# One query head group's transpose and the number of exp tiles in flight: a two-layer spectral and attention kernel

## The chip, the core and the metric

The kernel runs on one core of a Trainium2 chip. The metric is the device time of one execution in microseconds (us); the kernel before has a median of 1332.8 us over three runs (1332.57 to 1332.93). Engines are named as the profile names them: PE is TensorE (matmul), PEld its weight load, DVE is VectorE, ACT is ScalarE, POOL is GpSimd, SP is SyncE, which here only issues DMAs.

## What is computed

A residual stream of 2048 rows by 512 columns goes through two pairs of layers. A spectral layer normalises the rows, takes a 2-D real Fourier transform, multiplies by a complex filter and transforms back. An attention layer has 32 query heads of 16 columns each, and one key and one value head that all of them share.

```python
def _B_ref(x, wq, wk, wv, wo):
    H = 32; Dh = D // H
    q = (x @ wq).reshape(B, S, H, Dh).transpose(0, 2, 1, 3)
    k = x @ wk
    v = x @ wv
    scores = einsum("bhqd,bkd->bhqk", q, k) * (Dh ** -0.5)
    p = softmax(scores, axis=-1)
    o = einsum("bhqk,bkd->bhqd", p, v)
    return o.transpose(0, 2, 1, 3).reshape(B, S, H * Dh) @ wo

x = x + _A_ref(_layernorm(x), A_w_r, A_w_i)   # spectral
x = x + _B_ref(_layernorm(x), B_wq, B_wk, B_wv, B_wo)
x = x + _A_ref(_layernorm(x), A_w_r, A_w_i)
x = x + _B_ref(_layernorm(x), B_wq, B_wk, B_wv, B_wo)
```

## The kernel before

**Units of attention.** The 2048 queries are cut into four query blocks `qb` of 512. In each, the 32 heads are cut into four groups `g` of eight, and each group into two halves `par` of four heads: 4 x 4 x 2 = 32 *blocks* per layer. A block has 16 key chunks `kc` of 128 keys times 4 heads `h`, so 64 *units*. A unit is one score matmul (`scores`, L1341: 32 rows of the array, one 32-row strip per head, 128 keys by 512 queries), an exp of the 128x512 scores, and a product with the values (`pv`, L1363: 128 keys by 32 columns, one 32-column strip per head). Scores of heads in different strips run side by side, as do four products. Of the 32 columns of a value operand 16 are the values and 16 are constant, so that the product also gives the softmax's denominator.

**Who does the exp.** Two units at a time (a *pair*) go to ACT, which writes a 128x1024 tile `e` (`exp`, L1346). Single units go to DVE: `p1` (L1353) turns the score into the bits of a bf16 number by one multiply and add, an approximation of the exponential; four such units fill a tile, and two *phases* (`phase`, L1357 on POOL, L1359 on DVE) make shifted copies of it, so that such a unit has three products with weighted values instead of one.

**End of a block.** When all products of a block are in, DVE evacuates the accumulator with a transpose of its 32x32 squares (`evac`, L1370). After the second half of a group, DVE takes the reciprocals of the denominators (`recip`, L1375) and multiplies (`mul`, L1381), which leaves `on`, 128 queries' lanes by 512, in bf16. `on` has to be transposed back, in 32x32 squares, into `OT`, the operand of the output projection (`proj`, L1406). For all groups but the last of a layer this is `norm_dma` (L1392): four copies into a DRAM tile `onw` (L1401) and a DMA transpose out of it (L1402), all on SP's queue. For the last group it is `norm` (L1390), a transpose on DVE.

**Who decides the order.** All instructions are emitted by a planner (`Plan`), which keeps a clock for PE, ACT, DVE and POOL, with costs written in the code (`ACT_EXP = 908.0`, `DVE_P1 = 600.0`, and so on), and at each step emits the work that can start soonest. The order is therefore fixed when the program is built, per engine; on the chip each engine takes its own list in order and waits by semaphores. Which units go to ACT and which to DVE is decided there too, by whichever engine the plan sees going idle first (`deadline`, `do_scores`). A pair goes to ACT only if fewer than `self.bufs["ACT"]` exp tiles are live, that is, written or about to be, with products still to come:

```python
if kind == "ACT":
    if self.live["ACT"] >= self.bufs["ACT"] or self.slot_free("sa") is None:
        return False
```

`bufs["ACT"]` is `E_BUFS = 8` while a layer begins, and `E_LATE = 12` as soon as all values of the layer are there (L882). Up to `T_BUFS = 4` of DVE's tiles may be live. Within that, `peek` (L621) chooses heads for ACT's pair and DVE's unit so that they lie in different strips.

**Memory.** Exp tiles come from a ring of 21 fixed SBUF tiles `e2` (L975), which the spectral layer also uses: for its transposed input (`xt`, by DMA in the second pair, L1085), for the inverse transform's intermediate `V`, and for `Dz`, the sums and differences that `radix_d` (L1199) makes and the inverse transform's matmuls (`inv`, L1210) read.

Of the kernel before, what the change touches and what calls it, by code (L numbers as in the profile page):

```python
# [8 lines left out]
ACT = mybir.ActivationFunctionType  # L9
ALU = mybir.AluOpType  # L10
P = 128
BF = mybir.dt.bfloat16
# [40 lines left out]
    return tabs  # L53


def radix2(nc, o, x, piece):

    nc.vector.tensor_tensor(out=o, in0=x[:, 0:2, :], in1=x[:, 2:4, :], op=ALU.subtract if piece else ALU.add)


def radix4(nc, sd, x, half, o, piece):
# [53 lines left out]
class Plan:  # L115
# [12 lines left out]
    PORT = True  # L128
    POOL_LAG = 2600.0
    E_BUFS = 8  # L130
    E_LATE = 12
    T_BUFS = 4
    WIN = 3413.0
    WARM = 3500.0
# [11 lines left out]
    PATIENT = 1000.0  # L146
    URGE = 150.0
    TURN = 7000.0
    OUT_TURN = 25000.0
    EARLY_SD = 0  # L150
    STARVED = 12000.0

# [442 lines left out]
class Attn:  # L595
# [74 lines left out]
    def done(self, b, slot, end):  # L670
        p, em = self.plan, self.em
        qb, g, par = self.blocks[b]
        self.left.discard(b)
        m = Mark("PE", end, slot)
        ev = p.add("DVE", 630.0, [m], lambda k: em.evac(self, b, slot), give=(m,), prio=-3)
        self.evac[b] = self.evac_last = ev
        if par == 0:
            return
        tail = 0.0 if b >= len(self.blocks) - 2 else 5000.0
        rc = p.add("DVE", 260.0, [ev, self.evac[b - 1]], lambda k: em.recip(self, b), lazy=tail)  # L680
        mu = p.add("DVE", 600.0, [rc], lambda k: em.mul(self, b), lazy=tail, port=True)
        if b < len(self.blocks) - 2:
            no = Mark("DMA", None)

            def turned(k):
                em.norm_dma(self, b)
                no.end = k.end + p.OUT_TURN

            mu.then = turned
        else:  # L690
            no = p.add("DVE", 626.0, [mu], lambda k: em.norm(self, b), lazy=tail)
        self.evac[b] = no
        if g == 3:
            self.layer.close_rows(qb, [self.evac[8 * qb + 2 * i + 1] for i in range(4)])


class Layer:
# [83 lines left out]

    def add_middle(self):
        p, em = self.plan, self.em
        p.bufs["ACT"] = p.E_BUFS
        self.mid, self.fil = [], []
        for u in range(4):
            evs, two = [], u in self.two

            if two:
                outs = [((0, 2), (0, 1), 0), ((1, 3), (0, 1), 2)]  # L790
            else:
                outs = [((0, 1, 2, 3), (0, 1), 0), ((0, 1, 2, 3), (2, 3), 2)]
            if u % 2:
                outs = [(ts, (k,), o + i) for ts, ks, o in outs for i, k in enumerate(ks)]
            for ts, ks, o in outs:
                base, prev = None, []
                for t in ts:
                    deps, take = [self.g_done[t]] + prev, None
                    if not prev:
                        deps = deps + (self.gate if len(ks) == 2 else self.mm1_done[T - 1])  # L800
                        take = "sa" if len(ks) == 2 else "b"
                    k = p.add("PE", 434.0 * len(ks), deps, lambda k, u=u, ks=ks, t=t, ts=ts, base=base:
                              em.mid(self, u, ks, t, ts, (base or k).slot), take=take, order=10 + u)
                    base, prev = base or k, [k]
                evs.append(p.add("ACT", 909.0 if len(ks) == 2 else 482.0, prev, lambda k, u=u, o=o, n=len(ks), base=base:
                                 em.mid_evac(self, u, o, n, base.slot), give=(base,), order=10 + u))
            if two:
                evs = [self.pieces((600.0, 600.0), evs, lambda i, u=u: em.turn(self, u, i), 10 + u)]
            if u == 3 and not two:
                a = p.add("DVE", 1733.0, evs[:2], lambda k, u=u: em.filt(self, u, 0, 2), order=10 + u, port=True)  # L810
                mu = p.add("DVE", 1733.0, evs[2:] + [a], lambda k, u=u: em.filt(self, u, 2, 4), order=10 + u, port=True)
            else:
                mu = p.add("DVE", 3466.0, evs, lambda k, u=u: em.filt(self, u, 0, 4), order=10 + u, port=True)
            self.fil.append(mu)
            self.mid.append(self.pieces((600.0, 600.0), [mu], lambda i, u=u: em.radix_d(self, u, i), 26 if self.direct else 10 + u))
# [5 lines left out]
    def add_back(self):  # L821
        p, em, at = self.plan, self.em, self.at
        left = [T]
        for t in range(T):
            o = 20 + 10 * t
            cs = []
            for b in range(2):
                es = []
                for j in range(2):
                    if t == 0 and not self.direct:  # L830
# [3 lines left out]
                                  lambda k, t=t, b=b, j=j, m=m: em.inv(self, t, b, j, m.slot, (1,)), order=o)  # L834
                    elif t == 0:
# [3 lines left out]
                                  lambda k, b=b, j=j, m=m: em.inv0(self, b, j, m.slot, 1), order=o)  # L839
# [8 lines left out]
            for j in range(0, R, w):  # L848
                key, ks = ("b", t, j), []
                for i, r in enumerate(range(j, j + w)):  # L850
# [4 lines left out]
                    if put:  # L855
                        c = p.add("ACT", 482.0, [y], lambda k, t=t, r=r, y=y: em.put_x(t, r, y.slot), order=o + 1)
                        b = p.add("DVE", 795.0, [y], lambda k, key=key, i=i, t=t, r=r, w=w, y=y:
                                  em.bn(self, key, i, (t, r), w, y.slot), order=o + 2)
# [3 lines left out]
                    z = p.add("DVE", 597.0, [y], lambda k, t=t, r=r, y=y: em.add_x(t, r, y.slot), give=(y,), order=o + 1)  # L862
# [6 lines left out]
                for a in range(j, j + w, 2):  # L869
                    ap = [p.add("DVE", 323.0, [nb], lambda k, t=t, r=r: em.apply(self, t, r), order=o + 3) for r in (a, a + 1)]  # L870
                    x = p.add("PE", 560.0, ap, lambda k, s, t=t, a=a: em.tr_n(self, t, a, k.slot, s), parts=2, cols=1024.0, take="b", order=o + 4)
                    te.append(p.add(*self.flex(t, 893.0, 602.0), [x],
                                    lambda k, t=t, a=a, x=x: em.trn_evac(self, t, a, x.slot, k.eng), give=(x,), order=o + 4))
# [4 lines left out]
            def v_got(k, t=t):  # L878
                at.v_ready[t] = k.end + p.LAT[k.eng]
                left[0] -= 1  # L880
                if left[0] == 0:
                    p.bufs["ACT"] = p.E_LATE  # L882
                if left[0] == self.EARLY:
                    at.dve_on = True
                    at.dve_from = k.end - 2000.0
# [61 lines left out]
class Emit:  # L947


    def __init__(self, ctx, tc, ins, out):  # L950
        nc = self.nc = tc.nc
        A_x, self.w_r, self.w_i, B_wq, B_wk, B_wv, B_wo = ins
        mk = lambda nm, b=1, **kw: ctx.enter_context(tc.tile_pool(name=nm, bufs=b, **kw))
        const = mk("const")
# [17 lines left out]
        self.part = const.tile([P, 2], F32, name="part")  # L972
        self.wv = const.tile([P, NC, DH], BF, name="wv")
        self.tc = tc
        self.e2 = [const.tile([P, 1024], BF, name=f"e2_{i}") for i in range(21)]  # L975
        self.idle, self.home, self.writer = list(range(21)), {}, {}
        self.WO = const.tile([P, 4, D], BF, name="WO")
        self.junk = const.tile([P, 512], BF, name="junk")
        self.eps = const.tile([P, 1], F32, name="eps")
# [197 lines left out]
    def turn(self, L, u, piece):  # L1177
        if piece == 0:
            L.sd_of[("x", u)] = self.t4([4, 512])
        radix2(self.nc, L.sd_of[("x", u)][:, 2 * piece:2 * piece + 2, :], L.X[u], piece)  # L1180
        if piece:
            L.X[u] = L.sd_of.pop(("x", u))

# [14 lines left out]

    def radix_d(self, L, u, piece):  # L1199
        if piece == 0:  # L1200
            L.Dz[u] = [[self.t2([2, 512]), 4] for _ in range(2)]
            for z, _ in L.Dz[u]:
                self.writer.pop(self.home[id(z)][0], None)
        radix2(self.nc, L.Dz[u][piece][0], L.X[u], piece)

    def load_it(self, L, t):
        L.IT[t] = self.t4([4, 640], tag="it", bufs=2)
# [2 lines left out]
    def inv(self, L, t, b, j, slot, ks):  # L1210
        for v in range(T):
            if v <= t + 1 and v not in L.IT:
                self.load_it(L, v)
        ps = self.ps(slot).rearrange("p (u x) -> p u x", u=2)
        for k in ks:
            u = 2 * j + k
            for a in range(2):
                for i in range(2):
                    w = 128 * (3 - (t * a + i) % 4)
                    z = L.Dz[u][t % 2][0][:, a, 256 * i + 128 * b:256 * i + 128 * b + 128]  # L1220
                    self.nc.tensor.matmul(ps[:, k, :], lhsT=z, rhs=L.IT[t][:, u, w:w + 256], start=(a == 0 and i == 0),
                                          stop=(a == 1 and i == 1), skip_group_check=True)
            d = L.Dz[u][t % 2]
            d[1] -= 1
            if d[1] == 0:
                self.free2(d[0])

    def inv0(self, L, b, j, slot, k):

# [159 lines left out]
            at.OT[qb] = self.t4([4, 512])  # L1389
        self.nc.vector.transpose(out=at.OT[qb][:, g, :], in_=on.rearrange("p a h d -> p (a h d)"))  # L1390

    def norm_dma(self, at, b):  # L1392

        qb, g, par = at.blocks[b]
        on = at.raw.pop((qb, g))
        if g == 0:
            at.OT[qb] = self.t4([4, 512])
        way = self.way.tile([512, P], BF, name="onw", tag="onw")
        rows = way.rearrange("(a q) (h c) -> h q a c", q=32, c=32)
        for h in range(4):  # L1400
            self.nc.sync.dma_start(out=rows[h], in_=on[32 * h:32 * h + 32].rearrange("p a h d -> p a (h d)"))  # L1401
        self.nc.sync.dma_start_transpose(out=at.OT[qb][:, g:g + 1, :], in_=way)  # L1402

    def proj(self, at, t, r, slot, g0, g1):
        for g in range(g0, min(g1, 4)):
            self.nc.tensor.matmul(self.ps(slot), lhsT=at.OT[t][:, g, r * P:(r + 1) * P], rhs=self.WO[:, g, :],  # L1406
# [90 lines left out]
```

## Time and profile before

| | |
|---|---|
| median of three runs | 1332.8 us |
| profiled execution | 1332.57 us |
| its span, first to last instruction | 1330.8 us |
| POOL busy | 842.0 us (63%) |
| granted TensorE clock | 1.00 throughout |
| DMA | 33.05 MB; 6 to 9% of the 16 engines in most of the attention |
| first attention layer | from about 100 us to 675 us |
| second attention layer | from about 765 us to 1322 us |

The profile is of one execution. The busy time of an engine counts an instruction from its start to its end; consecutive instructions of DVE and ACT overlap by some tenths of a microsecond, so the time that an instruction takes away from its engine is the step from its start to the start of the next. In the rows of the tile view, the numbers behind the count are the shortest, median and longest duration in ns, then first and last start in us. The waits list who waited, at which line, for whom. The spectral layer at the start and between the attention layers leaves all engines partly idle; at 133 to 660 us and 800 to 1300 us PE, DVE and ACT are all near full.

### The profile page before, as it was taken

How to read it: one execution, taken by the hardware profiler on the slowest of the kernel's cores; microseconds unless marked ns; L12 is line 12 of the kernel's file. 1: busy time of each engine (PE TensorE's matmuls, PEld its weight loads, DVE VectorE, ACT ScalarE, POOL GpSimd, SP SyncE). 2: the span in 40 equal slices, each digit the busy share in tenths (PEclk: the TensorE clock that was granted, in tenths of full speed). 3: DMA queues.
4: the chain of work that ended last, by engine and by line, in shares of the span. 5: the costliest groups of instructions: out<-in, count | busy, mean ns of one | idle time of the engine just before them, and what ended most of it. 6: DMA issues, size and time to landing. Idle time of an engine off the chain costs nothing. (4 is left out here: it accounts for less than half of the span.)

```text
span 1330.8 us, 31765 instructions
## 1 busy us (share of the span) xinstructions
PE 1291.0 (97%) x12968; PEld 438.2 (33%) x13032; DVE 1273.3 (96%) x2280; ACT 1226.4 (92%) x1396; POOL 842.0 (63%) x826
## 2 busy tenths in 40 slices
PE   9999999999999999999999999999999999999998
PEld 4643222222222223332256422223222322322232
DVE  6998999999999999999979999999999999999998
ACT  6478999999999999999954899999999999999996
POOL 0004787857777667766720067887677867786785
PEclk9999999999999999999999999999999999999999
DMA  9100000010000100010051000000100010000001
GB/s 294 41 1 1 10 9 10 10 41 10 5 7 12 39 9 10 9 41 10 9 166 41 1 1 9 10 10 9 25 10 10 10 25 6 9 14 22 5 9 25
DMA packets 108722, 33.05 MB, mean 25 GB/s; under 512 B 88352, under 2 KB 107296, under 8 KB 108576
## 3 DMA queue, kind: packets, MB, share of 16 engines
q1 hardware_dynamic: 108288, 30.46, 10.0%
q8 instruction: 102, 1.67, 0.5%
q10 hardware_dynamic: 288, 0.56, 0.1%
q14 instruction: 44, 0.36, 0.1%
HBM read 17.89 MB, written 7.60 MB: 19 GB/s over the span
## 5 line engine op out<-in xcount | busy, mean ns | idle before, releaser
L1341 PEld LDWEIGHTS <-KA 32*128 32x128 bf16 x2048 | 87.6, 91 | 234.1 <-issue 222.9
L1341 PEld LDWEIGHTS <-KB 32*128 32x128 bf16 x2048 | 85.2, 91 | 229.7 <-issue 224.1
L1363 PEld LDWEIGHTS <-vs_116 128*32 128x32 bf16 x2474 | 98.3, 94 | 97.2 <-issue 90.8
L1363 PEld LDWEIGHTS <-vs_117 128*32 128x32 bf16 x1622 | 97.7, 94 | 62.8 <-issue 60.6
L1363 PEld LDWEIGHTS <-vs_118 128*32 128x32 bf16 x1622 | 71.0, 93 | 75.6 <-issue 72.8
L1363 PEld LDWEIGHTS <-vs_119 128*32 128x32 bf16 x1622 | 72.0, 94 | 65.5 <-issue 57.5
L1357 POOL INT64_ADD w_1388<-w_1387 x1 | 1.0, 1039 | 110.5 <-DVE w_1387 L1353 110.5
L1357 POOL INT64_ADD w_11001<-w_11000 x1 | 1.0, 1037 | 98.3 <-PE b_69 L1341 98.3
L1050 DVE BATCH_NORM_STATS2 st<-x_sb 128x6 f32<-128x512 bf16 x52 | 35.4, 681 | 4.1 <-DMA x_sb<-in_A_x_dram 3.6
L1346 ACT ACTIVATE e_8_92<-sa_65 128x1024 bf16<-128x1024 f32 x32 | 35.5, 1110 | 2.4 <-PE sa_64 L1341 1.6
L1346 ACT ACTIVATE e_6_90<-sa_64 128x1024 bf16<-128x1024 f32 x33 | 36.5, 1106 | 0.0
L1346 ACT ACTIVATE e_13_97<-sa_65 128x1024 bf16<-128x1024 f32 x31 | 34.7, 1118 | 1.6 <-PE sa_64 L1341 1.6
L1346 ACT ACTIVATE e_1_85<-sa_64 128x1024 bf16<-128x1024 f32 x32 | 35.4, 1107 | 0.0
L1346 ACT ACTIVATE e_5_89<-sa_65 128x1024 bf16<-128x1024 f32 x30 | 33.5, 1118 | 1.6 <-PE sa_64 L1341 1.6
L1346 ACT ACTIVATE e_12_96<-sa_65 128x1024 bf16<-128x1024 f32 x31 | 34.1, 1100 | 0.9 <-PE b_69 L1341 0.8
L1346 ACT ACTIVATE e_19_103<-sa_65 128x1024 bf16<-128x1024 f32 x31 | 34.7, 1121 | 0.1
L1346 ACT ACTIVATE e_10_94<-sa_65 128x1024 bf16<-128x1024 f32 x30 | 33.2, 1106 | 1.7 <-PE sa_64 L1341 1.6
L1346 ACT ACTIVATE e_18_102<-sa_64 128x1024 bf16<-128x1024 f32 x31 | 34.6, 1115 | 0.1
L1346 ACT ACTIVATE e_2_86<-sa_65 128x1024 bf16<-128x1024 f32 x30 | 33.5, 1116 | 1.3 <-PE sa_64 L1341 1.0
L1346 ACT ACTIVATE e_9_93<-sa_64 128x1024 bf16<-128x1024 f32 x31 | 34.6, 1115 | 0.1
L1346 ACT ACTIVATE e_7_91<-sa_65 128x1024 bf16<-128x1024 f32 x31 | 34.4, 1110 | 0.1
L1346 ACT ACTIVATE e_15_99<-sa_64 128x1024 bf16<-128x1024 f32 x31 | 34.3, 1107 | 0.1
(4100 smaller groups left out, 6438.4 us busy)
## 6 DMA issues: line engine op xcount, KB each, us to landing
it<-const_IT SPq DMA_DIRECT2D x8, 640.0 KB, 6.1
onw<-on SPq DMA_DIRECT2D x120, 32.0 KB, 1.9
x_sb<-in_A_x_dram SPq DMA_DIRECT2D x4, 512.0 KB, 6.8
out_dram<-x_sb SPq DMA_DIRECT2D x16, 128.0 KB, 1.9
way<-x_sb SPq DMA_DIRECT2D x6, 256.0 KB, 2.4
tab_PH<-const_PH ACTq DMA_DIRECT2D x1, 512.0 KB, 4.9
w_131<-const_FT SPq DMA_DIRECT2D x1, 512.0 KB, 8.8
w_136<-const_FT SPq DMA_DIRECT2D x1, 512.0 KB, 8.4
```

The costliest lines, as they stand in the source:

```text
L1050: self.nc.vector.bn_stats(st, self.ps(slot) if slot else self.x[:, x[1], x[0], :])
L1341: self.nc.tensor.matmul(o, lhsT=KX[rs, kc * P:(kc + 1) * P], rhs=at.QT[qb][rs, g, :], start=True, stop=True, skip_group_check=True)
L1346: self.wrote("ACT", e, self.nc.scalar.activation(out=e, in_=self.ps(slot), func=ACT.Exp, scale=SCALE))
L1357: self.nc.gpsimd.int64_add(t[p][:, 0:n].bitcast(U64), t[0][:, 0:n].bitcast(U64), DELTA[p] * FOUR)
L1363: self.nc.tensor.matmul(self.ps(slot)[32 * h:32 * h + 32, :], lhsT=V[:, kc, :], rhs=rhs, start=first, stop=last, skip_group_check=True)
```

## The change

The description of the change says that the score heads of ACT's pairs and DVE's tiles are chosen so that they lie in different strips. `peek`, which does so, is the same in both kernels. What differs is this. `norm_dma` is gone, and all groups are transposed by `norm` on DVE. `E_LATE` is gone, so that at most 8 exp tiles are live throughout. `Dz` has four tiles of its own (tag `xd`), and the shared ring has 13 tiles. `radix2` takes the whole tile and does the slicing itself.

```diff
-    E_LATE = 12
...
-    OUT_TURN = 25000.0
...
         mu = p.add("DVE", 600.0, [rc], lambda k: em.mul(self, b), lazy=tail, port=True)
-        if b < len(self.blocks) - 2:
-            no = Mark("DMA", None)
-
-            def turned(k):
-                em.norm_dma(self, b)
-                no.end = k.end + p.OUT_TURN
-
-            mu.then = turned
-        else:
-            no = p.add("DVE", 626.0, [mu], lambda k: em.norm(self, b), lazy=tail)
+        no = p.add("DVE", 626.0, [mu], lambda k: em.norm(self, b), lazy=tail)
         self.evac[b] = no
...
-        p.bufs["ACT"] = p.E_BUFS
...
-                if left[0] == 0:
-                    p.bufs["ACT"] = p.E_LATE
...
-        self.e2 = [const.tile([P, 1024], BF, name=f"e2_{i}") for i in range(21)]
-        self.idle, self.home, self.writer = list(range(21)), {}, {}
+        self.e2 = [const.tile([P, 1024], BF, name=f"e2_{i}") for i in range(13)]
+        self.idle, self.home, self.writer = list(range(13)), {}, {}
...
         if piece == 0:
-            L.Dz[u] = [[self.t2([2, 512]), 4] for _ in range(2)]
-            for z, _ in L.Dz[u]:
-                self.writer.pop(self.home[id(z)][0], None)
-        radix2(self.nc, L.Dz[u][piece][0], L.X[u], piece)
+            L.Dz[u] = self.t4([4, 512], tag="xd", bufs=4)
+        radix2(self.nc, L.Dz[u], L.X[u], piece)
...
-    def norm_dma(self, at, b):
-
-        qb, g, par = at.blocks[b]
-        on = at.raw.pop((qb, g))
-        if g == 0:
-            at.OT[qb] = self.t4([4, 512])
-        way = self.way.tile([512, P], BF, name="onw", tag="onw")
-        rows = way.rearrange("(a q) (h c) -> h q a c", q=32, c=32)
-        for h in range(4):
-            self.nc.sync.dma_start(out=rows[h], in_=on[32 * h:32 * h + 32].rearrange("p a h d -> p a (h d)"))
-        self.nc.sync.dma_start_transpose(out=at.OT[qb][:, g:g + 1, :], in_=way)
```

Because the planner's clocks change with the tasks, the whole order of scores, products and exps behind the first change is laid anew in the built program, on every engine.

More of the change, by code (lines that the diff above doesn't have):

```diff
@@ L53, in host_tables, with radix2 @@
     return tabs
-def radix2(nc, o, x, piece):
-    nc.vector.tensor_tensor(out=o, in0=x[:, 0:2, :], in1=x[:, 2:4, :], op=ALU.subtract if piece else ALU.add)
+def radix2(nc, sd, x, piece):
+    nc.vector.tensor_tensor(out=sd[:, 2 * piece:2 * piece + 2, :], in0=x[:, 0:2, :], in1=x[:, 2:4, :],
+                            op=ALU.subtract if piece else ALU.add)
 def radix4(nc, sd, x, half, o, piece):
@@ L1179, in turn @@
             L.sd_of[("x", u)] = self.t4([4, 512])
-        radix2(self.nc, L.sd_of[("x", u)][:, 2 * piece:2 * piece + 2, :], L.X[u], piece)
+        radix2(self.nc, L.sd_of[("x", u)], L.X[u], piece)
         if piece:
@@ L1219, in inv @@
                     w = 128 * (3 - (t * a + i) % 4)
-                    z = L.Dz[u][t % 2][0][:, a, 256 * i + 128 * b:256 * i + 128 * b + 128]
+                    z = L.Dz[u][:, 2 * (t % 2) + a, 256 * i + 128 * b:256 * i + 128 * b + 128]
                     self.nc.tensor.matmul(ps[:, k, :], lhsT=z, rhs=L.IT[t][:, u, w:w + 256], start=(a == 0 and i == 0),
                                           stop=(a == 1 and i == 1), skip_group_check=True)
[L1223 to L1226, printed above, removed]
     def inv0(self, L, b, j, slot, k):
```

## Prediction

> **What bounds the kernel now.** I read the page's busy line first, then the engines' busy times by stage, then the waits of the engine that the change loads.
>
> ```profile
> span 1330.8 us, 31765 instructions
> PE 1291.0 (97%) x12968; PEld 438.2 (33%) x13032; DVE 1273.3 (96%) x2280; ACT 1226.4 (92%) x1396; POOL 842.0 (63%) x826
> ```
>
> Three engines are nearly full, and an average cannot say which is nearest to its limit. So I take the two attention stretches alone (columns: stretch, length, then busy time of PE, PEld, DVE, ACT, POOL, the clock, the DMA share, GB/s):
>
> ```profile
> 140.00:660.00 520.00, 509.12 (x5307) 150.96 (x5329) 511.11 (x873) 517.07 (x572) 385.87 (x378) 1.00 0.09 15
> 800.00:1300.00 500.00, 489.83 (x5201) 147.28 (x5210) 491.03 (x822) 494.75 (x539) 383.02 (x370) 1.00 0.07 12
> ```
>
> VectorE has 520.00 - 511.11 = 8.9 us free in the first and 500.00 - 491.03 = 9.0 us in the second, 17.9 us together. ScalarE is as full (2.9 and 5.3 us free). Here whatever is added to either engine lengthens the stretch, unless it fits into these few microseconds or into work taken from the same engine. Where VectorE's free time goes, its waits say (each row: who, waited for whom, us in total, times, longest):
>
> ```profile
> DVE w_2777 L1285 <- PE b_69 L1325: 1.9, 1, 1.9
> DVE w_8863 L1353 <- PE sa_64 L1341: 1.6, 1, 1.6
> DVE w_14548 L1285 <- PE b_68 L1325: 1.9, 1, 1.9
> ```
>
> The long ones are single stalls in which TensorE makes query tiles (L1325) just ahead of the scores that need them. All VectorE waits in the two stretches add up to 7.1 and 7.8 us.
>
> **The DMA way of the head transpose.** The tile view of `on`, the normalised head group that is to be transposed:
>
> ```profile
> L1401 SPq DMA_DIRECT2D onw<-on x120: 315/489/1557, 145.2 to 1300.7; - x120
> L1381 DVE TENSOR_TENSOR on<-raw,rc x32: 676/682/694, 144.5 to 1322.7; 128x512 bf16<-128x512 f32 x32
> L1390 DVE STREAM_TRANSPOSE w_8479<-on x1: 711/711/711, 676.3 to 676.3; 128x512 bf16<-128x512 bf16 x1
> L1390 DVE STREAM_TRANSPOSE w_17903<-on x1: 712/712/712, 1323.5 to 1323.5; 128x512 bf16<-128x512 bf16 x1
> ```
>
> Of the 32 head groups (16 in each layer), 30 leave by DMA (120 copies, 30 DMA transposes on SP's queue) and 2, the last of each layer, are transposed on VectorE. The copies land in a median 1.9 us, the DMA transposes in 2.4 to 2.8 us, and the waits of TensorE, VectorE and ScalarE name no DMA inside the attention stretches: this path costs the bounding engines nothing today.
>
> **Part 1: 30 transposes return to VectorE.** The price is the step to the next start, not the duration, because VectorE overlaps the end of one instruction with the next. The timeline gives it:
>
> ```profile
> 142.72 0.68 DVE L1353 TENSOR_SCALAR w_1846<-b_68 128x512 uint16<-128x512 f32 x1
> 143.32 0.68 DVE L1353 TENSOR_SCALAR w_1846<-b_66 128x512 uint16<-128x512 f32 x1
> ...
> 660.16 0.71 DVE L1370 STREAM_TRANSPOSE raw<-b_68 128x512 f32<-128x512 f32 x1
> 660.79 0.65 DVE L1353 TENSOR_SCALAR w_9685<-b_69 128x512 uint16<-128x512 f32 x1
> ```
>
> An exp tile on VectorE (L1353) occupies 0.60 us, the evacuating transpose of equal width and duration (L1370) 0.63 us. The L1390 rows themselves are followed by waits, so their own step is not to be had; with 711 ns against 706 I give them 0.63. **30 x 0.63 = 18.9 us**, all in the full stretches. In exchange SP loses 150 DMAs. What stands behind them in its queue (the x blocks' way out and back, the stores) can only be issued sooner; no compute engine waits for those now, so the gain is 0. What this lets through next is nothing: VectorE stays the limit.
>
> One thing is not shown: an SBUF-to-SBUF transpose beside a running GpSimd add. Both L1390 rows ran with GpSimd idle. The rows beside it:
>
> ```profile
> 672.31 1.07 POOL L1357 INT64_ADD w_9851<-w_9849  x1
> 671.90 0.58 DVE L1359 TENSOR_SCALAR w_9889<-w_9888 128x512 uint16<-128x512 uint16 x1
> 672.40 1.12 DVE L1359 TENSOR_SCALAR w_9890<-w_9888 128x512 uint16<-128x512 uint16 x1
> ```
>
> The same 16-bit SBUF operation took 0.58 us once and 1.12 us while a GpSimd add ran to its end. At worst each transpose pays this 0.54 us: 30 x 0.54 = 16.2 us more. At best it pays nothing, as L1370 does (706 ns, step 0.63, in the 51 cases beside an add as in the 7 without), and that value I take, since L1390's 711 ns equals it. It can't be a gain, as the instructions do not exist today. The Trainium skill (VectorE: DVE Perf Modes, section "Two Vector instructions with no wait between them") has a one-input operation read through the interface shared with GpSimd only in a two-port mode; no row here shows which mode L1390 is in.
>
> The rule that speaks against all this is in the same page, sections "The three transpose paths" and "Rules for kernel authors": a 128x128 bf16 transpose takes 311 ns on VectorE and 1309 ns by DMA, and VectorE is called fastest for 32x32 blocks. By it, as an estimate, 30 x 4 x 1.0 = 120 us would be saved. The trace has 0.71 us for four times that width on VectorE and 2.4 us for a DMA landing, so the order of the two is the same, but no engine waits for the DMA and VectorE is full.
>
> **Part 2: 12 exp tiles in flight become 8.** This changes what the planner deals to whom, which the built order tells. Exp pairs on ScalarE (L1346): 1238 before, 1235 after. Exp tiles on VectorE (L1353): 1622 before, 1626 after. VectorE therefore gets 4 x 0.60 = **2.4 us** on top, while ScalarE loses 3 x 0.90 = 2.7 us (0.90 is the usual step between exps), which is off the path once VectorE is longer. This is the surprise of the built order. If the 18.9 us were shared, ScalarE would have to take some 10 pairs more, and each engine would end about 9 us later, at 1342. The planner does the reverse: with at most 8 live exp tiles ScalarE is not fed during the bursts in which VectorE finishes a group. Before, 36 exps had their first use 8 or more pairs later on TensorE; after, none has.
>
> TensorE: 7348 instead of 7340 head products (2 rounds, 0.4 us) and 59 more turns between scores, head products and full-width work. A round steps by 0.215 us, across a turn by 0.31, so 59 x 0.10 = 5.9 us. Warm-up products on zeros fall from 112 to 89, at most 1.7 us back. Net about +5 us, covered by the 21 us that the stretches grow; without that cover it would cost those 5 us.
>
> The last phase adds: VectorE makes 4 of one tile each before, and after one of four and two of two tiles. The two pairs took from 671.90 to 673.52 and the same at 1319, 3.2 us; eight tile widths at 0.50 (the first row's step) are 4.0, so **+0.8**, with -1 and +6 as ends (the whole width at the smallest step seen for the narrow form, or 1.12 us for each).
>
> **Part 3: four private tiles for the inverse transform's input; 13 shared tiles instead of 21.** The built order has the same 20 additions of the same shape. A shared tile comes round after 13 exps and is held for at most 8, so a writer finds it free (if it did not, it would wait one exp step, 0.90 us, each time): 0. The choice of strips by heads that the description names is not touched by the diff, so it brings no time.
>
> **VectorE's stalls.** They move with the plan. Counting TensorE work between VectorE's score tiles, by the steps above, the old order has eight places of 2.0 to 5.9 us, and the trace shows six stalls of 1.2 to 1.9 us; the new order has nine of 2.1 to 4.3 us. I keep 0, with -9 and +9 as ends (half of today's 17.9 us gone, or half as much again).
>
> **Sum.** 18.9 + 2.4 + 0.8 = 22.1 us. The profiled execution took 1332.57 us (span 1330.8 and 1.8 around it), 0.2 below the median of 1332.8. 1332.6 + 22.1 = 1354.7, and beside the median **1355**.
>
> **Rivals.**
> - *VectorE's free time takes it up (the other side).* The place is the 17.9 us in the two stretches, above all the query-tile stalls. For no change, 22.1 - 2.7 = 19.4 us would have to vanish, more than there is. If all of it went, 1336.8; if half, 1346. For: three engines plan anew, and the stalls are the planner's doing. Against: the new order has as many such places. Chance 0.10, of which 0.03 that the price of a transpose is also so much smaller that the time is within 0.2% of before or below.
> - *GpSimd disturbs the transposes.* 1355 + 16 = 1371. For: the 1.12 us row. Against: 711 ns looks like the undisturbed form. Chance 0.08.
> - *Eight in flight starve the rest.* The 36 late uses, held back one exp step each, are 36 x 0.90 = 32 us on ScalarE, which has 22.1 + 2.7 + 8.2 = 33 us free after the change. Should they fall where VectorE waits too, up to a third, some 10 us, is added: 1365. Chance 0.12.
> - *The change does nothing*: excluded by the built order.
>
> **How the numbers follow.** Forecast 0.70: 1348 to 1362. The rivals add 1337 to 1348 below, and 1362 to 1371 above. Leaving out the outer parts of both gives **1343 to 1368**. About 0.2% (2.7 us) is what can be told from no change here: slower 0.97, same 0.02, faster 0.01.
>
> **What would show it.** Right: VectorE 32 transposes at 0.71 us, its busy time near 1295 us and still about 98% of the attention stretches; ScalarE's free time there up by some 20 us; SP's queue nearly empty; each query-block period (141.7 us in layer two) longer by 2.5 to 3 us. Wrong: L1390's successors at 1.2 us, or VectorE with over 30 us free while ScalarE waits for TensorE, or ScalarE still full.

## The result, and the profile after

The changed kernel takes 1346.6 us (median of 4 runs, 1346.21 to 1348.28) against 1332.7 beside it: a ratio of 1.0107 (95% interval 1.0089 to 1.0124), 13.9 us slower. The time lies in the range that was given, on the side that was forecast; the likeliest case, 1355, was 8.4 us too high, and 1346.6 lies below the stretch of 1348 to 1362 that was given 0.70. It is where the rival "VectorE's free time takes it up" stood (1346, "if half"), with a chance of 0.10. The page's span and busy line of the changed kernel:

```profile
span 1344.3 us, 31506 instructions
PE 1303.0 (97%) x12950; PEld 442.1 (33%) x13017; DVE 1291.4 (96%) x2313; ACT 1224.3 (91%) x1393; POOL 843.7 (63%) x827
```

VectorE has 18.1 us more to do than before, ScalarE 2.1 us less. In the two attention stretches (columns as before: stretch, length, busy PE, PEld, DVE, ACT, POOL, clock, DMA share, GB/s):

```profile
140.00:667.00 527.00, 515.19 (x5305) 151.85 (x5324) 517.95 (x887) 515.34 (x570) 385.12 (x378) 1.00 0.03 8
807.00:1313.00 506.00, 495.74 (x5200) 149.61 (x5216) 500.47 (x838) 494.25 (x538) 385.04 (x372) 1.00 0.02 5
```

VectorE is free for 9.05 + 5.53 = 14.6 us (17.9 before), ScalarE for 11.66 + 11.75 = 23.4 us (8.2 before). VectorE has become the fuller of the two, and the room opened on ScalarE. The DMA share is down from 9 and 7% to 3 and 2%: the head groups' way through DRAM is gone.

The tile view of `on` (count, then shortest, median and longest ns) shows the transposes that came in:

```profile
L1362 DVE TENSOR_TENSOR on<-raw,rc x32: 675/682/694, 144.1 to 1337.2; 128x512 bf16<-128x512 f32 x32
L1371 DVE STREAM_TRANSPOSE w_1970<-on x4: 701/702/703, 149.7 to 257.3; 128x512 bf16<-128x512 bf16 x4
...
L1371 DVE STREAM_TRANSPOSE w_11507<-on x4: 701/702/704, 816.3 to 923.9; 128x512 bf16<-128x512 bf16 x4
```

**Where the 13.9 us lie.** To separate work from waiting I give each kind of VectorE instruction its usual step in an unbroken row (exp tile 0.598 for a duration of 0.681, evacuation 0.630, `mul` 0.599, `norm` 0.625, and so on), multiply by the counts, and call the sum VectorE's *list*. What the stretch takes beyond it is the *time above the list*: waits, and steps longer than usual. The stretch is from a layer's first exp tile on VectorE to its last evacuation, both layers together, in the profiled executions (1332.57 and 1346.21 us). All in us:

| | before | after | difference | forecast |
|---|---|---|---|---|
| VectorE's list in the attention | 1084.3 | 1104.9 | +20.6 | +22.1 |
| time above the list | 32.0 | 26.3 | -5.7 | 0 (ends -9 and +9) |
| ahead of the two attention stretches | 205.3 | 204.8 | -0.5 | 0 |
| after the last evacuation | 9.2 | 8.2 | -1.0 | 0 |

(The rounded rows sum to 13.4, against 13.6 of the two profiled executions.) The last row is the output projection's: the last group's transpose is followed by 13 projection matmuls in the trace before and by 7 in the one after, since the new plan does more of them ahead.

So two questions are open: is the list the thing that sets the time, and is the 5.7 us a share that any added work gets back, or chance of the new plan?

### The profile page after: what moved, and what is told of

Its sections match the earlier page's. It is cut to its first block, busy times and chain, and to the rows that moved or that the text cites. A ratio compares the mean times of both kernels' runs of the same rounds, so it can differ in the third digit from the quotient of the medians.

```text
span 1344.3 us, 31506 instructions
## 1 busy us (share of the span) xinstructions
PE 1303.0 (97%) x12950; PEld 442.1 (33%) x13017; DVE 1291.4 (96%) x2313; ACT 1224.3 (91%) x1393; POOL 843.7 (63%) x827
## 4 chain that ended last, share of the span: by engine, by line
ACT 60%; PE 22%; DVE 16%; issue 2%; DVEq 0%; ACTq 0%
ACT e_11_95 L1327 5%; ACT e_0_84 L1327 5%; ACT e_1_85 L1327 5%; ACT e_8_92 L1327 5%; ACT e_6_90 L1327 5%; ACT e_2_86 L1327 5%; ACT e_4_88 L1327 4%; ACT e_10_94 L1327 4%; ACT e_7_91 L1327 4%; ACT e_3_87 L1327 4%; ACT e_12_96 L1327 4%; ACT e_9_93 L1327 4%; ACT e_5_89 L1327 4%; PE b_67 L1344 2%; PE sa_65 L1322 2%
## 5 line engine op out<-in xcount | busy, mean ns | idle before, releaser
L1322 PEld LDWEIGHTS <-KB 32*128 32x128 bf16 x2048 | 88.5, 91 | 228.5 <-issue 221.8
L1344 PEld LDWEIGHTS <-vs_108 128*32 128x32 bf16 x2470 | 102.4, 93 | 97.7 <-issue 90.3
L1344 PEld LDWEIGHTS <-vs_109 128*32 128x32 bf16 x1626 | 97.1, 94 | 70.5 <-issue 69.0
L1344 PEld LDWEIGHTS <-vs_111 128*32 128x32 bf16 x1626 | 74.0, 94 | 79.0 <-issue 74.7
L1344 PEld LDWEIGHTS <-vs_110 128*32 128x32 bf16 x1626 | 71.6, 94 | 75.0 <-issue 70.6
L1327 ACT ACTIVATE e_8_92<-sa_65 128x1024 bf16<-128x1024 f32 x49 | 55.0, 1122 | 4.1 <-PE sa_64 L1322 4.1
L1327 ACT ACTIVATE e_6_90<-sa_65 128x1024 bf16<-128x1024 f32 x50 | 55.7, 1115 | 2.7 <-PE sa_64 L1322 2.5
L1327 ACT ACTIVATE e_7_91<-sa_65 128x1024 bf16<-128x1024 f32 x49 | 55.0, 1121 | 1.2 <-PE sa_64 L1322 1.0
L1327 ACT ACTIVATE e_12_96<-sa_65 128x1024 bf16<-128x1024 f32 x49 | 54.8, 1119 | 1.3 <-PE sa_64 L1322 0.9
L1327 ACT ACTIVATE e_11_95<-sa_64 128x1024 bf16<-128x1024 f32 x50 | 55.9, 1118 | 0.1
L1327 ACT ACTIVATE e_2_86<-sa_65 128x1024 bf16<-128x1024 f32 x46 | 51.8, 1127 | 4.4 <-PE sa_65 L1322 4.4
L1327 ACT ACTIVATE e_9_93<-sa_64 128x1024 bf16<-128x1024 f32 x49 | 54.8, 1118 | 0.8 <-PE b_69 L1322 0.8
L1327 ACT ACTIVATE e_4_88<-sa_65 128x1024 bf16<-128x1024 f32 x46 | 51.5, 1120 | 4.4 <-PE sa_64 L1322 3.5
L1327 ACT ACTIVATE e_3_87<-sa_65 128x1024 bf16<-128x1024 f32 x48 | 53.9, 1124 | 1.5 <-PE b_68 L1322 0.7
L1327 ACT ACTIVATE e_5_89<-sa_64 128x1024 bf16<-128x1024 f32 x49 | 55.0, 1121 | 0.1
L1327 ACT ACTIVATE e_5_89<-sa_65 128x1024 bf16<-128x1024 f32 x47 | 53.2, 1132 | 1.7 <-PE sa_64 L1322 1.4
L1327 ACT ACTIVATE e_2_86<-sa_64 128x1024 bf16<-128x1024 f32 x48 | 54.3, 1131 | 0.1
L1327 ACT ACTIVATE e_10_94<-sa_65 128x1024 bf16<-128x1024 f32 x48 | 54.1, 1128 | 0.0
L1327 ACT ACTIVATE e_0_84<-sa_65 128x1024 bf16<-128x1024 f32 x48 | 53.9, 1123 | 0.1
```

The lines of the kernel that those rows point to most:

```text
L1322: self.nc.tensor.matmul(o, lhsT=KX[rs, kc * P:(kc + 1) * P], rhs=at.QT[qb][rs, g, :], start=True, stop=True, skip_group_check=True)
L1327: self.wrote("ACT", e, self.nc.scalar.activation(out=e, in_=self.ps(slot), func=ACT.Exp, scale=SCALE))
L1344: self.nc.tensor.matmul(self.ps(slot)[32 * h:32 * h + 32, :], lhsT=V[:, kc, :], rhs=rhs, start=first, stop=last, skip_group_check=True)
```

## The experiments

Four theories. **A**: VectorE's list sets the time, and the time above it belongs to each plan. **B**: part of any added work, about a third, vanishes into VectorE's waits. **C**: the transposes carry all of the loss and eight in flight none. **D**: the long query-tile stalls cost nothing, because another wait is right behind them. In the table, units are exp tiles on VectorE and pairs those on ScalarE; the last two columns are measured as above.

| kernel | us | units / pairs | VectorE's list | above it |
|---|---|---|---|---|
| before | 1332.8 | 1622 / 1238 | 1084.3 | 32.0 |
| after | 1346.6 | 1626 / 1235 | 1104.9 | 26.3 |
| 1 transposes alone | 1340.8 | 1610 / 1243 | 1095.4 | 30.0 |
| 2 eight in flight alone | 1340.05 | 1636 / 1230 | 1092.7 | 29.8 |
| 3 extra transposes, old order | 1349.0 | 1622 / 1238 | 1106.1 | 27.5 |
| 4 transposes doubled, new order | 1365.6 | 1626 / 1235 | 1122.7 | 28.3 |
| 5 without the ring change | 1346.6 | 1626 / 1235 | 1104.9 | 26.3 |
| 6 before, query tiles earlier | 1329.5 | 1622 / 1237 | 1081.4 | 28.2 |
| 7 the same, with precedence | 1331.5 | 1612 / 1242 | 1074.9 | 35.8 |
| 8 after, query tiles earlier | 1335.7 | 1624 / 1236 | 1100.8 | 18.8 |
| 9 as 1, query tiles earlier | 1335.2 | 1600 / 1248 | 1086.5 | 34.2 |
| 10 as 2, query tiles earlier | 1334.1 | 1643 / 1227 | 1094.4 | 23.2 |
| 11 nine in flight, query tiles earlier | 1328.0 | 1630 / 1233 | 1086.2 | 23.6 |

The times are medians, the last two columns are of one execution each. Those of 3 and 4 took 1350.6 and 1366.6 us; in them TensorE's granted clock was 0.50 for 3.4 and 13.7 us, which adds some 1.6 and 5.5 us to the last column.

### 1. The transposes alone

The kernel before, with every group transposed on VectorE; 12 stay in flight.

```diff
-        if b < len(self.blocks) - 2:
+        if False:
```

> The kernel before, with every group's transpose on VectorE; 12 exp tiles in flight, 21 ring tiles and the DMA-free rest as before. The built order deals 1610 units to VectorE (1622 before) and 1243 pairs to ScalarE (1238), so VectorE's list grows by 30 x 0.625 - 12 x 0.598 = 11.6 us. Theory A (VectorE's list sets the time, and its stalls are a matter of each plan, zero on average): 1332.7 + 11.6 = 1344, give or take 5 for the stalls. Theory B (a third of whatever is added to VectorE disappears into its stalls, as 22 added gave 14): 1332.7 + 0.64 x 11.6 = 1340. Theory C (the transposes are what costs, and the 12 or 8 in flight do not matter): 1346.6, as the changed kernel.

1340.8 us, ratio 1.0059 (1.0044 to 1.0074): 8.0 us for 30 transposes whose steps sum to 18.75. The planner moved 12 units (7.2 us) off VectorE, so its list grew by only 11.1. This is the sharing that the prediction had worked out as "each engine would end about 9 us later, at 1342" and set aside, because the built order of the whole change doesn't show it. With 12 in flight it happens. A said 1344, give or take 5, and B 1340.

### 2. Eight in flight alone

```diff
-    E_LATE = 12
+    E_LATE = 8
```

> The kernel before with at most 8 exp tiles in flight throughout; transposes by DMA as before. The built order deals 1636 units to VectorE (1622 before) and 1230 pairs to ScalarE (1238): VectorE's list grows by 14 x 0.598 = 8.4 us. Theory A: 1332.7 + 8.4 = 1341, give or take 5. Theory B: 1332.7 + 0.64 x 8.4 = 1338. Theory C: 1333, no change.

1340.05 us, ratio 1.0065 (1.004 to 1.009): 7.2 us. Three executions took 1339.5 to 1340.6 us, the fourth 1347.0 at a mean granted clock of 0.992. C falls; A said 1341 and B 1338. The planner turned 8 pairs into 14 units (8.4 us) for VectorE; its list grew by 8.4. Parts 1 and 2 alone add up to 15.2 us, the whole measured 13.9.

### 3. Extra transposes in the old order

Each of the 30 groups that leave by DMA is also transposed on VectorE into a tile that nobody reads. It is emitted behind `mul`, out of the planner's sight, so the rest of the order stays as it was.

```diff
+        self.spare = const.tile([P, 512], BF, name="spare")
...
+        self.nc.vector.transpose(out=self.spare, in_=on.rearrange("p a h d -> p (a h d)"))
         way = self.way.tile([512, P], BF, name="onw", tag="onw")
```

> The kernel before in its own order, unit for unit, with 30 transposes of the same operand into a tile that nobody reads added to VectorE's list where the DMA way starts; the plan does not know of them. VectorE's list grows by 30 x 0.625 = 18.8 us and nothing else moves. Theory A: 1332.7 + 18.8 = 1351.5 within 2 us. Theory B: 1332.7 + 0.64 x 18.8 = 1345.

1349.0 us, ratio 1.012 (1.0103 to 1.0137), 16.1 us more. The tile view of `on` in this kernel:

```profile
L1399 DVE STREAM_TRANSPOSE spare<-on x30: 711/711/712, 145.7 to 1315.6; 128x512 bf16<-128x512 bf16 x30
L1391 DVE STREAM_TRANSPOSE w<-on x2: 711/711/711, 685.1 to 1341.2; 128x512 bf16<-128x512 bf16 x2
```

The added instructions have the duration of the two that were there before, but they cost more than the 0.625 that was expected for them. Each stands right behind the `mul` whose result it reads. VectorE's timeline at the first of them, before and in this kernel:

```profile
144.51 0.68 DVE L1381 TENSOR_TENSOR on<-raw,rc 128x512 bf16<-128x512 f32 x1
145.11 0.68 DVE L1353 TENSOR_SCALAR w_1906<-b_68 128x512 uint16<-128x512 f32 x1
```

```profile
144.98 0.68 DVE L1382 TENSOR_TENSOR on<-raw,rc 128x512 bf16<-128x512 f32 x1
145.70 0.71 DVE L1399 STREAM_TRANSPOSE spare<-on 128x512 bf16<-128x512 bf16 x1
146.33 1.85 DVE L1354 TENSOR_SCALAR w<-b 128x512 uint16<-128x512 f32 x3
```

The step of `mul` grows from 0.60 to 0.72, the transpose has 0.64, and the exp tile behind it 0.58 where it had 0.60: 0.73 us for each, 21.8 in all. So 74% of the added work came out as time. A's 1351.5 within 2 is missed by 2.5, and B's 1345 by 4; with the 21.8 us they would have said 1354.7 and 1346.9.

### 4. The transposes doubled in the new order

The changed kernel, with a second transpose into the spare tile behind each of the 32.

```diff
+        self.spare = const.tile([P, 512], BF, name="spare")
...
         self.nc.vector.transpose(out=at.OT[qb][:, g, :], in_=on.rearrange("p a h d -> p (a h d)"))
+        self.nc.vector.transpose(out=self.spare, in_=on.rearrange("p a h d -> p (a h d)"))
```

> The changed kernel in its own order, with each of the 32 transposes made twice, the second into a tile that nobody reads. VectorE's list grows by 32 x 0.625 = 20.0 us. Theory A: 1346.6 + 20.0 = 1366.6 within 2 us. Theory B: 1346.6 + 0.64 x 20.0 = 1359.

1365.6 us, ratio 1.024 (1.0225 to 1.0256), 19.0 us above the changed kernel. The second transposes are a little shorter, and their step is 0.593, so 19.0 us were added:

```profile
L1373 DVE STREAM_TRANSPOSE spare<-on x32: 667/669/673, 151.1 to 1359.0; 128x512 bf16<-128x512 bf16 x32
```

It would be wrong to read this as 100%. Three of the four executions had a mean granted clock of 0.995 or 0.996, where the changed kernel's 1346.6 has 1.000. The profiled one is of these, and the loss is in one place (length, busy PE, PEld, DVE, ACT, POOL, clock, DMA share, GB/s):

```profile
828.50:842.20 13.70, 13.70 (x95) 2.35 (x95) 9.16 (x15) 9.26 (x10) 7.42 (x8) 0.50 0.01 2
```

TensorE loses 6.9 us of full clock here, and VectorE waits for it: set beside the same instructions of the changed kernel, VectorE's are 5.5 us later behind this stretch than ahead of it. The one execution at 0.999 took 1362.2 us, 15.6 above the changed kernel, which is 82% of the 19.0. So in fixed orders 74% (3) and 82% (4) of the added work come out as time. A (1366.6 within 2) and B (1359) both miss: a third is too much, but between a fifth and a quarter does vanish, in the old plan as in the new one. 82% rests on a single execution.

### 5. Without the ring change

The kernel before with `E_LATE = 8` and all transposes on VectorE, but with its ring of 21 tiles and `Dz` in the ring.

> The changed kernel without its third part: transposes on VectorE and 8 in flight, but the ring of 21 tiles and the inverse transform's input in the ring, as before. The built order is that of the changed kernel on every engine, but for the names of tiles. If the ring costs nothing: 1346.6 within 1. If the shorter ring makes exps wait for their tile: below 1345.

1346.6 us (1346.29 to 1348.11), ratio 1.0107 (1.009 to 1.0124), the same as the changed kernel. Part 3 costs nothing, as priced, and the loss is that of parts 1 and 2.

### 6. Query tiles earlier, in the kernel before

The prediction named the query-tile stalls as the largest of VectorE's. Here the tiles may be made six blocks ahead instead of three.

```diff
-            while self.qt_todo and 8 * self.qt_todo[0][1] + 2 * self.qt_todo[0][0] - b <= 3:
+            while self.qt_todo and 8 * self.qt_todo[0][1] + 2 * self.qt_todo[0][0] - b <= 6:
```

> The kernel before, with the query tiles put on the planner's list up to six blocks ahead of their use in place of three (the condition <= 3 becomes <= 6). VectorE gets 1622 units as before; two pairs of query-tile copies move from VectorE to ScalarE in the lead-in. In the built order the five places where query tiles stand just ahead of VectorE's next score are three (4.8, 4.6 and 3.5 us of TensorE work, where before had one of 5.9 and four of 4.0). Theory A (list plus stalls, and stalls are such places): the four stalls of 1.9 us go and one or two of some 2 us come, 1332.9 - 4 = 1329 (1326 to 1331). Theory D (the stalls only move, VectorE's excess over its list stays at its 32 us): 1333.

1329.5 us, ratio 0.9976 (0.9966 to 0.9986). D falls. 3.3 us come back: 2.9 as a shorter list and 3.8 from above it, less 2.1 ahead of the two stretches, where 15 query-tile matmuls in place of 7 now precede each layer's first exp tile on VectorE, and 1.1 behind the last evacuation.

### 7. The same, query tiles with precedence

```diff
-        ... take="b", prio=2, order=order, ...        # qt_mm
+        ... take="b", prio=-2, order=order, ...
```

> As the run with query tiles six blocks ahead, and the planner also gives them precedence (prio -2 in place of 2). VectorE gets 1612 units, ten fewer, which is 10 x 0.598 = 6.0 us off its list; ScalarE gets 1242 pairs, four more. The built order has seven places of 2.6 to 5.9 us of TensorE work between VectorE's scores (before: eight of 2.0 to 5.9). Theory A: 1332.9 - 6 = 1327, give or take 4. Theory D with the list's share alone: 1327 as well, within 1. A theory by which TensorE or ScalarE is as near to its limit as VectorE: 1331 or more, since ScalarE is given 3.6 us more.

1331.5 us, ratio 0.999 (0.9981 to 1.0). VectorE's list is 6.5 us shorter than in 6, yet the kernel is 2.0 us slower: the time above the list rose by 7.6. Here the same sum for ScalarE (0.904 a pair, 0.48 to 0.57 for its evacuations) leaves only 22.4 us above it, less than in any other kernel: 31.7 before, 48.4 after. A as I had written it, with VectorE's list alone, is too narrow. That ScalarE is as full and so holds the time up fits this, but no run adds work to ScalarE alone.

### 8. Query tiles earlier, in the changed kernel

The edit of 6 in the changed kernel.

> The changed kernel with the query tiles put on the planner's list six blocks ahead in place of three. VectorE gets 1624 units (1626), and four query-tile copies fall out of its attention stretches: 1.2 + 2.4 = 3.6 us off its list. The built order has six places of 2.1 to 3.6 us of TensorE work between VectorE's scores, where the changed kernel has nine of 2.1 to 4.3. If such places make the stalls: 1346.6 - 3.6 - 3 = 1340. If VectorE's time above its list has a floor at the 26 us that the changed kernel shows: 1343. If the stalls in the changed kernel are query tiles as in the one before (where this edit brought 3.3 us): 1343 too, by another way; then the waits of the query-tile copies fall from 2.3 us to none and others stay.

1335.7 us, ratio to before 1.0025 (1.0015 to 1.0034): 10.9 us of the 13.9 are undone, more than any theory had. The windows over the two attention stretches of this kernel:

```profile
111.30:677.80 566.50, 558.69 (x5779) 165.16 (x5777) 561.22 (x957) 556.61 (x614) 418.21 (x409) 1.00 0.04 12
772.30:1325.50 553.20, 547.63 (x5742) 160.78 (x5740) 548.49 (x918) 544.46 (x592) 422.01 (x407) 1.00 0.01 4
```

VectorE is free for 5.3 + 4.7 us of 1119.7, the fullest of all plans: 18.8 us above its list, against 26.3. The list fell by 4.1. The transposes are still all on VectorE, so the loss of the change is no fixed price of its instructions; the order in which they are dealt weighs as much. Against 6, the kernel before with the same edit, the change still costs 6.2 us.

### 9 and 10. Each part alone, query tiles earlier

9 is kernel 1, and 10 kernel 2, each with the edit of 6. This completes all eight combinations of the two parts and that edit.

> The kernel before with both: every transpose on VectorE, 12 exp tiles in flight, and the query tiles six blocks ahead. VectorE gets 1600 units (1622 before), ScalarE 1248 pairs (1238). VectorE's list: 30 x 0.625 - 22 x 0.598 - 2.4 for four copies = +3.2 us; ScalarE's: +9.0 us. The built order has five places of 5.4 to 6.6 us between VectorE's scores, more than any other. List with unchanged stalls: 1336. With these places as stalls of 3 to 4 us: 1340. ScalarE as the limit (its list plus the 22 us above it that the tightest run so far shows): 1333 + 9 - 9 = 1333.

> The kernel before with 8 exp tiles in flight and the query tiles six blocks ahead; transposes by DMA. VectorE gets 1643 units (1622 before): its list grows by 21 x 0.598 - 2.9 = 9.7 us. The run with both and the transposes on VectorE stood 18.8 us above its list, where the kernel before stands 32.0 and the one with earlier query tiles and 12 in flight 28.2. If 8 in flight is what lets the query tiles' earlier place pay: 1332.8 + 9.7 - 13 = 1329. If the transposes on VectorE are what fills the stalls (they can be done while TensorE is away): 1332.8 + 9.7 - 4 = 1338.

1335.2 (ratio 1.0021, 1.0012 to 1.0031) and 1334.1 (1.0011, 1.0001 to 1.002). 9 comes out where the list with unchanged stalls put it (1336); 10 lies between its two theories (1329 and 1338), so neither is borne out. The times in us:

| | DMA, 12 | VectorE, 12 | DMA, 8 | VectorE, 8 |
|---|---|---|---|---|
| query tiles 3 blocks ahead | 1332.8 | 1340.8 | 1340.05 | 1346.6 |
| query tiles 6 blocks ahead | 1329.5 | 1335.2 | 1334.1 | 1335.7 |

The transposes on VectorE cost 8.0, 6.5, 5.7 and 1.7 us, depending on the rest; eight in flight costs 7.2, 5.8, 4.6 and 0.5. No cell gives a price that holds in the others. One thing does hold in all four: from 12 to 8, VectorE's list grows (by 8.4, 9.5, 13.0 and 14.3 us) and the time above it falls (by 2.2, 3.7, 5.0 and 15.4).

### 11. Nine in flight, query tiles earlier

The kernel before with `E_LATE = 9` and the edit of 6, transposes by DMA.

> The same with 9 in flight. VectorE gets 1630 units: its list grows by 8 x 0.598 - 2.9 = 1.9 us. The built order has only two places of over 2.2 us between VectorE's scores (5.2 and 4.4), the fewest of all. If such places make the time above the list, it is the smallest here too, 18 us: 1332.8 + 1.9 - 14 = 1321. If the transposes are what fills the stalls: 1332.8 + 1.9 - 4 = 1331.

1328.0 us (1327.58 to 1328.29), ratio 0.9963 (0.9948 to 0.9978): faster than both kernels. It is also 1.5 us below 6, but on another chip and with ratios whose intervals overlap. I had hoped for 1321 from counting the places where TensorE does other work between VectorE's score matmuls: this order has two of them, kernel 8 has six. Yet the time above the list is 23.6 here and 18.8 there, so the count does not predict it.

## Why the prediction was right, and where it was not

**What bounds the kernel: right, within a limit.** In a fixed order (3, 4) work added to VectorE comes out as time at 74 and 82%, not in full. Two other engines are as near to their limit. Kernel 7 fits ScalarE as a second bound. TensorE, busy for 97% of the span, is a third: in the half-clock stretch of 4 some 80% of what it lost came out as delay (5.5 of 6.9 us). The prediction counted 5 us more work for TensorE as covered by the longer stretches; no run tests this term by itself.

**Part 1, 30 x 0.63: right.** The step is 0.625. The unknown beside it, the SBUF transpose beside a GpSimd add, is settled at the lower end. In the changed kernel's timeline of VectorE, then of GpSimd (columns: start, us, engine, line, operation, tiles):

```profile
187.57 0.70 DVE L1371 STREAM_TRANSPOSE w_1970<-on 128x512 bf16<-128x512 bf16 x1
188.19 0.65 DVE L1266 CAST w_2545<-b_66 128x512 bf16<-128x512 f32 x1
```

```profile
187.23 1.04 POOL L1338 INT64_ADD w_2498<-w_2497  x1 [0.66 <-DVE w_2497 L1334]
188.24 1.04 POOL L1338 INT64_ADD w_2499<-w_2497  x1
```

The transpose lies inside an add (187.23 to 188.27) and takes its 0.70 us, 0.62 to the next start; the add takes its usual 1.04. In 30 of the 32 an add ran beside the transpose for at least 0.2 us, and all of these took 0.69 to 0.71 us. The rival "GpSimd disturbs the transposes" (1371) falls.

**Part 2, 4 x 0.60: right** for this plan. Kernel 1 shares the transposes' cost with ScalarE, and kernel 2 shows that it is the lower limit that gives VectorE work. That it does so because ScalarE is not fed during VectorE's bursts is argued from the built order, not shown. But the prediction read the two parts as 18.9 and 2.4. Measured alone they are 8.0 and 7.2 us: of the loss, about half is the limit of eight's. The sum of VectorE's list was right because it was made from the built order as a whole.

**The last phases, +0.8: mis-sized, it is -0.2.** After the change they are one operation of four tiles' width and two of two:

```profile
680.47 1.57 DVE L1340 TENSOR_SCALAR w_9793<-w_9791 128x2048 uint16<-128x2048 uint16 x1
...
1333.86 1.13 DVE L1340 TENSOR_SCALAR w_19229<-w_19228 128x1024 uint16<-128x1024 uint16 x1
1334.91 0.41 DVE L1340 TENSOR_SCALAR w_19230<-w_19228 128x1024 uint16<-128x1024 uint16 x1
```

From the first's start to the last's end these are 1.57 and 1.46 us, 3.04 together, against 3.24 before. (In the list they count -0.6, as their steps hold the evacuation's wait for the last products, 1.8 us before and 1.4 after.) The 0.50 for a width was no price of the operation: GpSimd's adds stood in its way. GpSimd's timeline, before (the next add is shown in the prediction) and after:

```profile
671.29 1.04 POOL L1357 INT64_ADD w_9850<-w_9849  x1 [0.34 <-DVE w_9849 L1353]
```

```profile
680.46 1.04 POOL L1338 INT64_ADD w_9792<-w_9791  x1 [0.35 <-DVE w_9791 L1334]
1333.67 1.04 POOL L1338 INT64_ADD w_19197<-w_19195  x1
```

An add is running when the phase starts in all of these rows but the last (1334.91), and the phase ends a fixed time after that add, whenever it began: 0.15 us for one width (672.48 after 672.33, 673.52 after 673.38), 0.28 for two (1334.99 after 1334.71) and 0.54 for four (682.04 after 681.50). So the prediction's 0.58 was not the undisturbed row that it was read as, and one wide operation that waits for one add is cheaper than two that wait for two.

**"VectorE's stalls ... I keep 0": the step that failed**, in size. Of the 8.5 us between forecast and profile, 5.7 are here, 1.5 in the list and 1.5 outside the attention (rounded). They gave back 5.7 us, inside the ends of -9 and +9. The prediction compared eight places with TensorE work between VectorE's scores against nine, and took the like count for a like cost; and it held that whatever is added to an engine lengthens the stretch. The waits of VectorE in the second attention stretch of the changed kernel (who, waited for whom, us in total, times, longest):

```profile
DVE w_12082 L1266 <- PE b_66 L1306: 1.3, 1, 1.3
...
DVE x_sb L1257 <- PE b_66 L1375: 0.6, 1, 0.6
...
DVE w_14495 L1266 <- PE b_67 L1306: 0.4, 1, 0.4
```

The query-tile copies (L1285 before, L1266 now) waited 1.9 us three times in that layer before, now 1.3 and 0.4. In both attention layers these waits fell from 9.6 to 2.3 us. Others took part of it back (all of VectorE's waits there: 21 us before, 18 after; the rest of the 5.7 are steps that came nearer to the usual one); in the first layer VectorE's longest wait is now for scores that stand behind the next layer's matmuls:

```profile
DVE w_6236 L1334 <- PE sa_64 L1322: 2.9, 1, 2.9
```

**"VectorE's free time takes it up": partly true.** A quarter of the added list (5.7 of 20.6, 28%) came back from above it. Kernels 3 and 4, whose orders are fixed, give back 26 and 18% of what is added, which for 20.6 us would be 3.7 to 5.4. So most of the 5.7 can be the share that any added work gets back, and the prediction gave this rival too little; what is then left to the new plan is at most 2 us. That plans differ by far more is shown by 7 and 8. That the time fell inside the range owes something to luck: the range reached so far down only because of this rival, which was thought unlikely.

**"Eight in flight starve the rest": refuted as a loss on top.** ScalarE does wait more, as that rival said:

```profile
ACT e_4_88 L1327 <- PE sa_64 L1322: 3.5, 1, 3.5
ACT e_8_92 L1327 <- PE sa_64 L1322: 2.9, 1, 2.9
ACT e_6_90 L1327 <- PE sa_64 L1322: 1.5, 1, 1.5
```

These are its longest in the second stretch; before, three of 1.6 us were. But ScalarE had the room (23.4 us free after the change), and the time above VectorE's list fell in all four pairs of 12 and 8 in flight.

**The signs that were named.** 32 transposes at 0.70, VectorE busy 1291.4 us (about 1295 forecast) and 98.3 and 98.9% of the stretches, ScalarE's free time up by 15 (20 forecast), the queue of SP nearly empty: as said. A query block grew by 8.7 / 4 = 2.2 us in the first layer and 6.2 / 4 = 1.6 in the second, where 2.5 to 3 was said; that is the failed term.

**What stays open.** Why a plan has 18.8 or 35.8 us above VectorE's list is not settled. That fewer exp tiles in flight make ScalarE less full, and so let both engines wait less for the same TensorE products, fits all four pairs and kernel 7, but is argued, not shown; the count of places in the built order failed in 11.

## What to carry to other kernels

In a kernel whose order a planner makes, price an edit as the bounding engine's list in the built order plus the time above it, and take the second as a property of the plan: here an edit of the planner alone took it from 26.3 to 18.8 us (8), and another from 28.2 to 35.8 (7). Even in a fixed order do not expect all of an added step: three quarters to four fifths came out here, with three engines near their limits. A part's cost measured alone is the part plus what the planner deals anew: cross the parts (two by two, and once more with an unrelated edit of the order) before giving either a price. Work that waits on an idle queue, here head transposes that went by DMA, is free as long as no engine waits for it; bringing it to an engine that is 98% full costs up to its step, less what is dealt away and what the waits give back: here 1.7 to 8.0 us for 18.75 us of steps.

## What the runs showed of the hardware

`mul`, a VectorE operation with two SBUF inputs, lengthens a GpSimd add beside it and not itself. In the changed kernel's timelines of VectorE and of GpSimd:

```profile
183.98 0.68 DVE L1362 TENSOR_TENSOR on<-raw,rc 128x512 bf16<-128x512 f32 x1
```

```profile
184.16 1.40 POOL L1338 INT64_ADD w_2453<-w_2452  x1 [0.35 <-DVE w_2452 L1334]
```

`mul` takes its 0.68 us, and the add that starts 0.18 us into it takes 1.40 instead of 1.04; in 27 such cases it took 1.32 to 1.40. The Trainium skill (SBUF — State Buffer, section "Who interferes with whom") has it that an operation with at most one SBUF input, outside the two-port modes, leaves GpSimd alone and one with two does not, where GpSimd's instruction reads SBUF: both agree with the rows here, the transpose with one input and `mul` with two. It also says that in a two-port mode the later of the two is blocked outright. The 16-bit operation of the phases behaves so: in the rows above it ended 0.15, 0.28 and 0.54 us after the end of the add that was running at its start, for widths of 512, 1024 and 2048, and where no add was running 128x1024 took 0.41 us. Its mode itself is in no row.
